# A softcap attention and maxout kernel: a fourth U buffer, and the reciprocal's transfers and multiplications moved in the written order

## The chip, the cores and the metric

The kernel runs on one core of a Trainium2 chip. The metric is the device time of one launch in microseconds (us), from start to end on that core. The time before is the median of three runs, and the profile is of one more execution of the same kernel.

In the profile the engines are called PE (the matrix engine), DVE (the vector engine), ACT (the scalar engine), POOL (GpSimd) and SP (the engine that issues nearly all transfers here). "SPq" is SP's instruction queue: its entries are the issues of transfers, not the transfers themselves.

## The reference

Two stages follow each other. The first is attention with a soft cap on the scores, for 8 batches of 12 heads with 448 rows of 64; the second is a layer on its 3584 rows of 768 that takes the larger of two products and multiplies it once more.

```python
scores = (1 / sqrt(64)) * (q @ k.T)
scores = cap * tanh(scores / cap)                  # cap = 30
attn = exp(scores - max(scores)); attn = attn / (sum(attn) + 1e-9)
x = (attn @ v)                                     # heads side by side: 3584 x 768
out = maximum(x @ w1, x @ w2) @ w_out              # 768 -> 1024 -> 768
```

## The kernel before

**Tiling.** Two heads make a pair (128 partitions), so there are N = 48 pairs, numbered i. Three pairs make a group g (16 groups), which is the unit of loading, casting and transposing. Two pairs make an iteration t of the main loop (line 523, NQ = 24 iterations); pair i = 2t is its first half, pair 2t + 1 its second. A "slot" in the text is such a half, numbered as the pairs are.

**Attention.** For each iteration PE makes the scores of the next one (`scores`, line 277), ACT takes tanh and then exp of them, both into bf16, and PE multiplies the exponentials with v (`pv`, line 325). Nothing is divided yet: `pv` copies the product to a float32 tile `U[t]` (line 351, on DVE) and the sums of the exponentials, which PE forms in `ss`, to a tile `st` (line 354). There are three buffers for U.

**The reciprocal's way.** The sums stand in rows of a 128 x 448 tile. A small transfer (the *gather*, line 357) packs them into 32 x 56, DVE takes the reciprocal (`invert`, line 363), a second transfer writes the result to memory (`rec_d`, line 365), and two more read it back, repeated over 64 partitions each (`spread`, line 371, `rec_b`). At last POOL multiplies U by rec_b into xT, the bf16 input of the second stage (`normalize`, line 383). So one iteration's reciprocal takes three stages of transfers, all issued from SP's queue, and each of them waits there for the one before.

**Loads and transposes.** From group 4 on, q and k of a group are loaded in float32 (`load`, lines 137 to 148), cast by POOL to bf16 in a tile kqf (`cast`), and turned by one crossbar transfer per group (`cross`, line 268) into qkT, which `scores` reads. v is loaded and cast. The groups before 4 are turned by PE (`transposes`).

**The second stage** (`moe`, line 388) is a generator for one batch: each step is one matmul. The main loop draws such steps between its own work with F(n), and the weights are made ready in the same way in iterations 1 to 4 (`turn_w2`, `premultiply`, and `subtract` on DVE). When the main loop is over, the rest of the steps run alone.

**What sets the order.** The kernel has a manual schedule: each engine, and SP's queue too, runs its instructions in the order in which the program writes them, and waits in front of each until what it needs is there. A list `todo` (lines 455 to 476) says in which slot a load, cast or transpose is written; `extra(i)` writes what is listed for slot i. With e = 3g for even g and 3g - 1 for odd g, k is loaded in slot e - 8 and q there or, for odd g, one slot on; they are cast in e - 6; the transpose and v's load stand in e - 4, v's cast in e - 2. In the steady state this gives a round of three iterations:

- iterations 5, 8, 11, 14, 17: a transpose, a v, a k and a q in one slot (called *heavy* below);
- iterations 6, 9, 12, 15, 18: a k and, half an iteration on, a q (*light*);
- iterations 7, 10, 13, 16, 19: a transpose and a v (*middle*).

Around these, an iteration t over 4 writes, in this order: spread(t - 2), extra(2t), pv(t, 0), normalize(t - 2), invert(t - 1), extra(2t + 1), and pv(t, 1) with the gather of t.

Of the kernel before, what the change touches and what calls it, by code (L numbers as in the profile page):

```python
# [10 lines left out]
def kernel(  # L11
# [11 lines left out]
    nc = tc.nc  # L23
    f32 = mybir.dt.float32
# [4 lines left out]
    B, H, S, D = q.shape  # L29
# [3 lines left out]
    P = 128  # L33
# [4 lines left out]
    NQ = N // 2  # L38
    Q0 = 4 * P
    NJ = 3  # L40
    NT = 4
# [7 lines left out]
    upool = ctx.enter_context(tc.tile_pool(name="upool", bufs=2))  # L49
# [227 lines left out]
    def scores(t, p, m0=0, m1=2):  # L277

        if m0 == 0:
            tanh[t, p] = att.tile([P, 4, S], bf16, name="tanh")  # L280
        if p == 2:
            s = s_psum.tile([P, 2, 512], f32, name="s")
        for m, (ab, j) in list(enumerate(PARTS[p]))[m0:m1]:
            i = 2 * t + ab
            g = i // L
            k0 = qkT[g][:, i % L, :, :].rearrange("p j c -> p (j c)")
            o = Q0 + (64 * (i // NP % 2) if g >= NT else 0)
            qTn = k0[:, o : o + S]
            if p == 2:
                nc.tensor.matmul(s[:, m, :S], k0[:, 3 * P : 4 * P], qTn)  # L290
                continue
            s = s_psum.tile([P, 2, 512], f32, name="s")
            for h in range(2):
                r = slice(64 * h, 64 * h + 64)
                nc.tensor.matmul(s[:, h, :S], k0[r, j * P : (j + 1) * P], qTn[r, :])  # L295
            nc.scalar.activation(tanh[t, p][:, 2 * m : 2 * m + 2, :], s[:, :, :S], AF.Tanh, scale=scale / cap)  # L296
        if p == 2:
            nc.scalar.activation(tanh[t, p][:, 0:2, :], s[:, :, :S], AF.Tanh, scale=scale / cap)  # L298

    def ex(t, p):  # L300
        n = 2 if p == 2 else 4
        expo[t, p] = att.tile([P, n, S], bf16, name=f"expo{p}", bufs=1 if p == 3 else 2)
        nc.scalar.activation(expo[t, p], tanh[t, p][:, 0:n, :], AF.Exp, scale=float(cap))  # L303

    def e_of(t, ab, j):
        p, m = LP[ab, j]
        return expo[t, p][:, m : m + (1 if j == NJ else 2), :]
# [3 lines left out]
    def add(t, ab, step):  # L311

        if t < NS or t >= NQ:
            return
        if t not in esum:
            esum[t] = att.tile([P, 4, S], bf16, name="esum")
        d = esum[t][:, 2 * ab : 2 * ab + 2, :]
        if step == 0:
            nc.vector.tensor_add(d, e_of(t, ab, 1 if ab else 0), e_of(t, ab, 2 if ab else 1))  # L319
        else:  # L320
            nc.vector.tensor_add(d, d, e_of(t, ab, 0 if ab else 2))  # L321

    U, sums, rec, recd = {}, {}, {}, {}

    def pv(t, ab):


        i = 2 * t + ab
        g, n = divmod(i, L)
        ps = pv_psum.tile([P, 512], f32, name="pv")  # L330
        for j in range(NJ):
            for h in range(2):
                r = slice(64 * h, 64 * h + 64)
                nc.tensor.matmul(  # L334
                    ps[r, :S], vp[g % 2][:, 2 * n + h, j, :], e_of(t, ab, j)[:, h, :], start=(j == 0), stop=False
                )
        if ab:
            ss = pv_psum.tile([P, 512], f32, name="ss")
            for m in range(2):
                nc.tensor.matmul(  # L340
                    ss[64 * m : 64 * m + 64, :S], ones2, expo[t, 2][:, m, :], start=True, stop=False
                )
            nj = NJ if t < NS else 1
            for j in range(nj):
                for m in range(4):
                    x = e_of(t, m // 2, j)[:, m % 2, :] if t < NS else esum[t][:, m, :]
                    nc.tensor.matmul(ss[32 * m : 32 * m + 32, :S], ones, x, start=False, stop=(j == nj - 1))  # L347
        nc.tensor.matmul(ps[:, :S], vl[g % 2][:, n, :], expo[t, 2][:, ab, :], start=False, stop=True)  # L348
        if ab == 0:
            U[t] = upool.tile([P, 2, S], f32, name="u", bufs=3)  # L350
        nc.vector.tensor_copy(U[t][:, ab, :], ps[:, :S])  # L351
        if ab:
            st = upool.tile([P, S], f32, name="st", bufs=1)
            nc.vector.tensor_copy(st, ss[:, :S])

            sums[t] = xpool.tile([32, 56], f32, name="sums")
            nc.sync.dma_start(
                out=sums[t], in_=st.rearrange("(m p) (a c) -> m p a c", p=32, a=8)[:, 0, :, :]
            )
# [7 lines left out]
    def spread(t):  # L367
        rec[t] = xpool.tile([P, 2, S], f32, name="rec_b")
        lines = recd[t].rearrange("(n h a) c -> h n (a c)", h=2, a=8)
        for h in range(2):  # L370
            nc.sync.dma_start(
                out=rec[t][64 * h : 64 * h + 64, :, :], in_=lines[h : h + 1, :, :].to_broadcast([64, 2, S])
            )
# [3 lines left out]
    def normalize(t, ab, eng=nc.gpsimd):  # L377
        i = 2 * t + ab
        b, hp = divmod(i, NP)
        if i % (2 * NP) == 0:  # L380
            xT[b // 2] = xpool.tile([P, NP, 2 * S], bf16, name="xT")
        cs = slice((b % 2) * S, (b % 2 + 1) * S)
        eng.tensor_mul(xT[b // 2][:, hp, cs], U[t][:, ab, :], rec[t][:, ab, :])  # L383
# [55 lines left out]
    def F(n):  # L439
        while n > 0 and fill_q:  # L440
            try:
                next(fill_q[0])
                n -= 1
            except StopIteration:
                fill_q.pop(0)
# [6 lines left out]
    def at(i, f, *a):  # L452
        todo[i].append((f, a))

    for g in range(2, NL):
        if g < NT:
            e = 0 if g == 2 else 1
            at(3 * g - 6 + e, load, g, "k")
            at(3 * g - 6 + e, load, g, "q")
            at(3 * g - 4 + e, load, g, "v")  # L460
            at(3 * g - 4, cast, nc.gpsimd, g, "k")
            at(3 * g - 4, cast, nc.gpsimd, g, "q")
            at(3 * g - 2, cast, nc.gpsimd, g, "v")
        else:
            e = 3 * g - g % 2
            at(e - 8, load, g, "k")
            at(e - 8 + g % 2, load, g, "q")
            at(e - 6, cast, nc.gpsimd, g, "k")
            at(e - 6, cast, nc.gpsimd, g, "q")
            at(e - 4, cross, g)  # L470
            at(e - 4, load, g, "v")
            at(e - 2, cast, nc.gpsimd, g, "v")
    at(1, load, 1, "v")
# [39 lines left out]
    def weights(i):  # L513
        if MS <= i < MS + KC:
            fill_q.append(turn_w2(i - MS))
        if MS < i <= MS + KC:
            fill_q.append(premultiply(i - MS - 1))

    def extra(i):
        for f, a in todo[i]:  # L520
            f(*a)

    for t in range(NQ):
        i = 2 * t
        more = t + 1 < NQ
        more8 = 1 if t >= 8 and more else 0
        weights(i)
        if t % 3 == 2 and t > 2:
            fill_q.append(moe(t // 3 - 1))
        if more:  # L530
            scores(t + 1, 0)
        ex(t, 3)
        F(2)
        add(t, 0, 1)
        F(2)
        if i + 3 < NT * L:
            transposes(i + 3)
        F(5 + more8 if more else 0)
        if t > 4:
            spread(t - 2)  # L540
        extra(i)
        F(6 if more else 3)
        if more:
            scores(t + 1, 1)
            ex(t + 1, 0)
        pv(t, 0)
        F(8 + more8)
        F(3 if more else 0)
        if MS < i <= MS + KC:
            subtract(i - MS - 1)  # L550
        if t > 4:
            normalize(t - 2, 0)
            normalize(t - 2, 1)
        if more:
            scores(t + 1, 2)
            ex(t + 1, 1)
        weights(i + 1)
        if i + 4 < NT * L:
            transposes(i + 4)
        F(2 + more8 if more else 0)  # L560
        add(t, 1, 0)
        F(4 if more else 2)
        add(t, 1, 1)
        F(2 if more else 0)
        if t > 4:
            invert(t - 1)
        elif t > 1:
            spread(t - 2)
        extra(i + 1)
        F(3 + more8 if more else 0)  # L570
        if more:
            scores(t + 1, 3)
            ex(t + 1, 2)
        pv(t, 1)
        F(4)
        if more:
            add(t + 1, 0, 0)
        F(3 if more else 0)
        if 0 < t < 5:
            invert(t - 1)  # L580
        if 1 < t < 5:
            normalize(t - 2, 0)
            normalize(t - 2, 1)
        if MS < i + 1 <= MS + KC:
            subtract(i - MS)
    F(6)
    spread(NQ - 2)
    F(10)
    invert(NQ - 1)
    F(16)  # L590
    spread(NQ - 1)
# [40 lines left out]
```

## Time and profile before

| what | value |
|---|---|
| median of three runs | 379.54 us (375.2 to 382.09) |
| span of the profiled execution | 379.2 us |
| mean granted PE clock | 0.980 of full speed |
| DVE busy | 200.6 us (53%) |
| ACT busy | 281.8 us (74%) |
| POOL busy | 150.1 us (40%) |
| transfers issued by SP | 71.1% of 16 engines' time, 67.99 MB |
| a u copy on DVE (line 351) | 624 ns, 48 of them |
| a multiplication on POOL (line 383) | 1238 ns, 48 of them |

How to read it: ACT's work ends with the last exponential at about 319 us; after that PE runs the remaining steps of the second stage alone. Up to there each iteration needs about 12 to 13 us. The share of a busy engine is an average over the start (loads and PE transposes), the middle (attention with matmul steps between) and the end (matmul steps alone), and these have different limits. The number of matmuls is fixed by the program, so an idle PE in the middle is time that isn't won back at the end.

### The profile page before, as it was taken

Reading aid. Unit: us, or ns where it says so; the run is one execution under the profiler, and the core shown is the slowest. Engines: PE = TensorE matmul, PEld = TensorE weight load, DVE = VectorE, ACT = ScalarE, POOL = GpSimd, SP = SyncE. Lnnn points to the kernel's source line nnn. Section 1 sums busy time; section 2 is a strip of 40 time slices with the busy share of each in tenths; the row PEclk is TensorE's granted clock in tenths of the full one; section 3 lists DMA queues with packets and bytes.
Section 4 is the critical chain, followed back from the end, with each engine's and each line's share of the span. In section 5 each row is a group of like instructions: output and inputs, shape, how many; then the busy total and the mean of one; then the engine's idle time right before and its main releaser. Section 6 shows DMA issues by size and latency. Waiting matters only on the chain.

```text
span 379.2 us, 6549 instructions
## 1 busy us (share of the span) xinstructions
PE 349.0 (92%) x2492; PEld 168.2 (44%) x2492; DVE 200.6 (53%) x348; ACT 281.8 (74%) x265; POOL 150.1 (40%) x188
## 2 busy tenths in 40 slices
PE   3677986898999999999999999999989999999996
PEld 2223443443444444444444454434434444555563
DVE  4223473567665676455745654557448556633421
ACT  4999986697999989998898899889958897000000
POOL 3734135637554445444562456243644302420000
PEclk9997898999999999999999999999989999999999
DMA  7999999996788987999698959896988132422022
GB/s 251 263 209 220 274 284 223 227 193 139 215 212 221 213 232 203 223 234 255 177 213 208 251 163 250 232 242 165 216 217 213 51 91 105 122 80 95 2 83 84
DMA packets 104464, 71.56 MB, mean 189 GB/s; under 512 B 58224, under 2 KB 99440, under 8 KB 104432
## 3 DMA queue, kind: packets, MB, share of 16 engines
q1 hardware_dynamic: 102480, 67.99, 71.1%
q0 software_dynamic: 1952, 3.15, 4.5%
q8 instruction: 19, 0.31, 0.4%
q14 instruction: 13, 0.11, 0.1%
HBM read 53.48 MB, written 11.18 MB: 171 GB/s over the span
## 4 chain that ended last, share of the span: by engine, by line
PE 65%; DMA 19%; DVE 5%; SPq 4%; ACT 3%; issue 2%; POOL 1%; POOLq 0%; DVEq 0%; ACTq 0%
PE mm L396 17%; PE mm L411 16%; PE mm L408 12%; PE pv L334 6%; DMA qkT<-kqf 6%; PE s L295 6%; DMA qr<-in_q_dram 6%; DMA vr<-in_v_dram 4%; DMA rec_b<-rec_d 3%; PE pv L348 3%; PE ss L347 2%; PE s L290 1%; DVE u L351 1%; ACT expo L303 1%; ACT tanh L296 1%
## 5 line engine op out<-in xcount | busy, mean ns | idle before, releaser
L296 ACT ACTIVATE tanh<-s 128x896 bf16<-128x896 f32 x144 | 124.3, 915 | 32.5 <-PE s L295 31.1
L303 ACT ACTIVATE expo<-tanh 128x1792 bf16<-128x1792 bf16 (+1 forms) x96 | 144.9, 1510 | 0.1
L383 POOL TENSOR_TENSOR xT<-u,rec_b 128x448 bf16<-128x448 f32 x48 | 58.4, 1238 | 101.1 <-DMA rec_b<-rec_d 81.2
L411 PE MATMUL mm<-wo_sb,gT 128*128 128x384 bf16 x448 | 86.8, 330 | 0.0
L396 PE MATMUL mm<-xT,wd_sb 128*128 128x448 bf16 x384 | 79.1, 354 | 2.7 <-POOL xT L383 1.3
L351 DVE COPY u<-pv 128x448 f32<-128x448 f32 x48 | 29.9, 624 | 91.0 <-PE pv L348 78.3
L408 PE MATMUL mm<-wm_sb,xT 128*128 128x384 bf16 x336 | 66.6, 326 | 0.2 <-DVE gT L400 0.2
L411 PEld LDWEIGHTS <-gT 128*128 128x128 bf16 x448 | 43.6, 99 | 31.1 <-issue 3.6
L415 DVE COPY osb<-mm 128x384 f32<-128x384 f32 x56 | 31.1, 555 | 46.3 <-PE mm L411 46.0
L396 PEld LDWEIGHTS <-wd_sb 128*128 128x128 bf16 x384 | 37.2, 98 | 38.4 <-issue 5.9
L295 PE MATMUL s<-qkT 64*128 64x448 bf16 x288 | 43.2, 371 | 11.1 <-ACT tanh L298 3.4
L400 DVE TENSOR_SCALAR gT<-mm 128x448 bf16<-128x448 f32 x64 | 39.1, 616 | 16.8 <-PE mm L396 16.6
L408 PEld LDWEIGHTS <-xT 128*128 128x128 bf16 x336 | 32.5, 98 | 23.3 <-issue 1.9
L334 PE MATMUL pv<-expo,vp 128*64 128x448 bf16 x288 | 37.5, 370 | 0.0
L158 POOL CAST vp<-vr 128x1152 bf16<-128x1152 f32 x15 | 18.0, 1201 | 46.8 <-DMA vr<-in_v_dram 43.5
L321 DVE TENSOR_TENSOR esum<-esum,expo 128x896 bf16<-128x896 bf16 x38 | 29.9, 787 | 1.5
L319 DVE TENSOR_TENSOR esum<-expo 128x896 bf16<-128x896 bf16 x38 | 26.6, 699 | 0.0
L295 PEld LDWEIGHTS <-qkT 64*128 64x128 bf16 x288 | 9.4, 95 | 36.8 <-issue 28.7
L298 ACT ACTIVATE tanh<-s 128x896 bf16<-128x896 f32 x24 | 22.0, 917 | 4.4 <-PE s L290 3.9
L334 PEld LDWEIGHTS <-vp 128*64 128x64 bf16 x288 | 12.4, 110 | 21.3 <-issue 15.2
L232 PE MATMUL mm<-wo_sb,w2T 128*128 128x384 bf16 x96 | 19.1, 334 | 1.4 <-DVE qkT L264 1.4
L178 POOL CAST kqf<-qr 128x1152 bf16<-128x1152 f32 x12 | 14.5, 1207 | 9.6 <-DMA qr<-in_q_dram 9.4
(56 smaller groups left out, 227.7 us busy)
## 6 DMA issues: line engine op xcount, KB each, us to landing
rec_b<-rec_d SPq DMA_DIRECT2D x48, 224.0 KB
kr<-in_k_dram SPq DMA_DIRECT2D x12, 576.0 KB
qr<-in_q_dram SPq DMA_DIRECT2D x12, 576.0 KB
vr<-in_v_dram SPq DMA_DIRECT2D x12, 576.0 KB
out_dram<-osb SPq DMA_DIRECT2D x17, 384.0 KB
out_dram<-osb SPq DMA_DIRECT2D x22, 192.0 KB
osb<-in_moe_w_dram SPq DMA_DIRECT2D x6, 512.0 KB
vr<-in_v_dram SPq DMA_DIRECT2D x8, 288.0 KB
```

Of the source, the lines that this page charges most:

```text
L295: nc.tensor.matmul(s[:, h, :S], k0[r, j * P : (j + 1) * P], qTn[r, :])
L296: nc.scalar.activation(tanh[t, p][:, 2 * m : 2 * m + 2, :], s[:, :, :S], AF.Tanh, scale=scale / cap)
L303: nc.scalar.activation(expo[t, p], tanh[t, p][:, 0:n, :], AF.Exp, scale=float(cap))
L321: nc.vector.tensor_add(d, d, e_of(t, ab, 0 if ab else 2))
L334: nc.tensor.matmul(ps[r, :S], vp[g % 2][:, 2 * n + h, j, :], e_of(t, ab, j)[:, h, :], start=(j == 0), stop=False)
L351: nc.vector.tensor_copy(U[t][:, ab, :], ps[:, :S])
L383: eng.tensor_mul(xT[b // 2][:, hp, cs], U[t][:, ab, :], rec[t][:, ab, :])
L396: nc.tensor.matmul(ps[:, :S], wd_sb[:, c, f * P : (f + 1) * P], x[:, c, cs], start=(c == 0), stop=(c == KC - 1))
L400: nc.vector.tensor_relu(g[:, f, cs], ps[:, :S])
L408: nc.tensor.matmul(ps[:, : DM // 2], x[:, c, ts], wm_sb[:, c, hs], start=(c == 0), stop=False)
L411: nc.tensor.matmul(ps[:, : DM // 2], g[:, f, ts], wo_sb[:, f, hs], start=False, stop=(f == FC - 1))
L415: nc.vector.tensor_copy(osb[:, hs], ps[:, : DM // 2])
```

## The change

Five edits to buffers and to the written order; no operation on data is added or taken away.

1. `upool` gets a fourth buffer for U, so that iteration t's first copy waits for the multiplication of t - 4 and not of t - 3.
2. Group 4's k and q are loaded in slot 5 and cast in slot 7, where before they were in 4 and 6. For odd groups from 5 on, q is loaded in the same slot as k and not one slot on.
3. `cross` is written first in the loop over groups. For groups that share a slot the order is by group, before and after.
4. spread(t - 1) is written right ahead of the second pv of iteration t, and so ahead of that iteration's gather; before, it was written in iteration t + 1, behind the gather.
5. normalize(t - 2) is written ahead of extra(2t), so that POOL multiplies before it casts; before it came behind. Iterations 2 to 4 and the end are fitted to this.

It is meant to bring the reciprocals sooner, so that POOL doesn't stand still with casts queued behind a multiplication, and to free DVE from waiting for a U buffer.

```diff
         if ab == 0:
-            U[t] = upool.tile([P, 2, S], f32, name="u", bufs=3)
+            U[t] = upool.tile([P, 2, S], f32, name="u", bufs=4)
...
             e = 3 * g - g % 2
-            at(e - 8, load, g, "k")
-            at(e - 8 + g % 2, load, g, "q")
-            at(e - 6, cast, nc.gpsimd, g, "k")
-            at(e - 6, cast, nc.gpsimd, g, "q")
+            first = g == NT
             at(e - 4, cross, g)
+            at(e - 8 + first, load, g, "k")
+            at(e - 8 + first, load, g, "q")
+            at(e - 6 + first, cast, nc.gpsimd, g, "k")
+            at(e - 6 + first, cast, nc.gpsimd, g, "q")
             at(e - 4, load, g, "v")
             at(e - 2, cast, nc.gpsimd, g, "v")
...
+        if t == 4:
+            spread(t - 2)
         if t > 4:
-            spread(t - 2)
+            normalize(t - 2, 0)
+            normalize(t - 2, 1)
         extra(i)
...
-        if t > 4:
+        if t == 4:
             normalize(t - 2, 0)
             normalize(t - 2, 1)
...
         if t > 4:
             invert(t - 1)
-        elif t > 1:
+        elif 1 < t < 4:
             spread(t - 2)
         extra(i + 1)
         F(3 + more8 if more else 0)
         if more:
             scores(t + 1, 3)
             ex(t + 1, 2)
+        if t > 4:
+            spread(t - 1)
         pv(t, 1)
...
         if 0 < t < 5:
             invert(t - 1)
-        if 1 < t < 5:
+        if t == 4:
+            spread(3)
+        if 1 < t < 4:
             normalize(t - 2, 0)
             normalize(t - 2, 1)
...
-    F(6)
-    spread(NQ - 2)
-    F(10)
+    F(16)
     invert(NQ - 1)
```

## The prediction

> **What bounds the kernel now.** I read the page's busy times and slices first, then PE's timeline for its idle stretches, then what ended them on DVE, and last SP's own queue and its waits.
>
> ```profile
> PE 349.0 (92%) x2492; PEld 168.2 (44%) x2492; DVE 200.6 (53%) x348; ACT 281.8 (74%) x265; POOL 150.1 (40%) x188
> PE   3677986898999999999999999999989999999996
> PEclk9997898999999999999999999999989999999999
> DMA  7999999996788987999698959896988132422022
> ```
>
> PE is busy 349.0 of 379.2 us. From about 90 us on it hardly stops: in windows of 20 us it is busy 20.00 four times between 100 and 200, and all its idle time between 100 and 320 us adds up to 3.5 us. The 48 matmuls of line 396 that start at 325.45 take 9.08 us, 189 ns each, so this busy PE is at its full rate. What can be won lies in the few idle pieces, and in the clock dips beside them.
>
> ```profile
> 64.47 0.90 PE L262 MATMUL mm<-ident,kqf 64*64 64x64 bf16 x26 [3.66 <-DVE wm_sb L237]
> 88.21 0.35 PE L396 MATMUL mm<-xT,wd_sb 128*128 128x448 bf16 x1 [1.26 <-POOL xT L383]
> 277.61 0.55 PE L295 MATMUL s<-qkT 64*128 64x448 bf16 x4 [1.85 <-DMA qkT<-kqf]
> 63.33 0.62 DVE L351 COPY u<-pv 128x448 f32<-128x448 f32 x1 [5.60 <-POOL xT L383]
> 260.73 0.49 DVE L363 RECIPROCAL rec_s<-sums 32x56 f32<-32x56 f32 x1 [0.40 <-DMA sums<-st]
> ```
>
> The bracket is the idle time in front, and what ended it. The fourth line explains the first: DVE stood 5.60 us at iteration 3's first u copy, because three U buffers made it wait for POOL's first multiplication, and PE's next PSUM tile was behind that on DVE. The last line matters most: in iteration 18 the reciprocal is already reached by DVE before its gather has landed.
>
> ```profile
> 241.62 1.27 SPq L371 DMA_DIRECT2D rec_b<-rec_d  x2
> 242.99 4.64 SPq L268 DMA_TRANSPOSE qkT<-kqf  x1
> 247.68 0.57 SPq L137 DMA_DIRECT2D vr<-in_v_dram  x1
> 248.30 1.29 SPq L148 DMA_DIRECT2D vr<-in_v_dram  x2
> 249.63 0.60 SPq L137 DMA_DIRECT2D kr<-in_k_dram  x1
> 250.28 1.26 SPq L148 DMA_DIRECT2D kr<-in_k_dram  x2
> 251.59 0.60 SPq L137 DMA_DIRECT2D qr<-in_q_dram  x1
> 252.23 0.99 SPq L142 DMA_DIRECT2D qr<-in_q_dram  x1
> 253.32 1.13 SPq L431 DMA_DIRECT2D out_dram<-osb  x1
> 254.55 0.73 SPq L365 DMA_DIRECT2D rec_d<-rec_s  x1
> 255.37 0.61 SPq L357 DMA_DIRECT2D sums<-st  x1
> 260.50 1.26 SPq L371 DMA_DIRECT2D rec_b<-rec_d  x2
> ...
> SPq L371 <- DMA rec_d<-rec_s: 31.4, 14, 4.4
> POOL xT L383 <- DMA rec_b<-rec_d: 81.2, 20, 9.5
> ```
>
> This is SP in a heavy iteration. It issues without a pause from 241.62 to 255.98, then stands 4.5 us until rec_d has landed (31.4 us over the run). The spreads of the heavy iterations start at 103.34, 143.01, 181.79, 221.19 and 260.50: a round of three iterations takes 39.3 us. In the round 202.79 to 241.62 (38.8 us) SP's pauses are only 3.7 (for rec_d), 0.6 (for st) and 1.9 (for rec_d), so 32.7 us is issuing. SP is the second resource without slack: at 230.61 and 269.47 the transposes go out so late that PE waits 0.45 us at 237.5 and 1.85 us at 277.6. POOL's 81.2 us of waiting cost PE little, for POOL has 60% of the span free.
>
> **What the Trainium skill says.** "DMA: Bandwidth & Descriptors", in "Anatomy of one DMA", gives about 2.0 us as a transfer's fixed cost (for the GpSimd path) and says that a wait is taken by the issuing sequencer before dispatch, not by the DMA engines; so everything behind it in the queue waits too. The trace agrees: nothing is issued in the 4.5 us before 260.50. The same page, "Queues, rings and completion order", says that each engine takes descriptors in ring order, so a 7 KB write stands behind the loads issued before it. Here rec_d of 254.55 was free to be read back only at 260.50, and the DMA engines were 90% busy up to about 257.5. "TensorE: Matmul & The Clock Gate", "What's actually happening", says that the clock is halved after an idle window of about 3.4 us. After the 3.66 us pause the 26 small transposes took 0.90 us, against 0.60 at 54.89; after the 1.85 us pause eight matmuls of line 411 took 2.56 us, against 1.30 elsewhere, though that pause is shorter than the page's window.
>
> **The change part by part.**
>
> The fourth U buffer and group 4's later load: iteration 3's copy no longer waits. DVE gets 5.60 us, PE 3.66 us of idle and about 1.3 us of slow clock (0.3 on the transposes, 0.75 on the four matmuls of line 232 behind them, the rest on line 221). Spread(0) goes out ahead of 1.3 MB of group 4, so it lands before the 60.1 us of now. The 1.26 us at 88.21 goes too, as normalize(2) is written half an iteration sooner. Sum: 5 to 7 us sooner by iteration 5, if SP follows. The 0.6 us that later first multiplications could cost POOL lie beside its free 60%.
>
> cross first in the loop over groups: the slot lists are unchanged by it, since each slot is still ordered by group. Nothing. The q load of odd groups moves ahead of rec_d in the light iterations; the same issue time, 1.25 us.
>
> normalize ahead of the casts: POOL's two multiplications take 2.2 us and wait for nothing now, as their spread was issued half an iteration before. Casts start up to 4 us sooner, but they are done about 10 us ahead of their transpose already (group 14's at 260.7, its transpose at 269.47). Nothing on the path.
>
> spread ahead of the gather: the added wait. SP now issues rec_d(t - 1) and then stands until it has landed, with the gather of t, the next iteration's transpose and its loads queued behind. Before, a q load (1.3), the gather (0.6) and sometimes an output (0.5 to 1.5) lay in that time. Latency from the end of rec_d's issue to the spread: heavy 3.9, 4.4, 3.75, 4.45, 5.2, mean 4.3; middle 2.15, 3.0, 3.2, 2.9, mean 2.8; light at most 2.7, 4.4, 4.2, 3.8. For the light one I take 3.0, between the 2.0 of the skill's page and the 4.4. Sum 10.1 us a round against 6.2 now. Issue time: 32.7, or 30.8 if each entry took its shortest seen time; I take 31.7, since longer rounds leave the rings emptier. Round: 31.7 + 10.1 = 41.8 us. Both ends, with the shortest and the longest latencies (3.75 + 2.0 + 2.15 and 5.2 + 4.4 + 3.2): 30.8 + 7.9 = 38.7 and 32.7 + 12.8 = 45.5.
>
> Who waits: the gather goes out behind the spread, so iteration t + 1's reciprocal waits, and DVE stands in front of it with PSUM copies behind it, so PE stops a moment later. Direct check, with all else as now: the gathers of the heavy iterations would go out at 104.6, 144.3, 183.5, 222.5 and 261.8 and land 2 to 3.5 us later; DVE now takes these reciprocals at 107.1, 145.0, 183.3, 220.4 and 260.7. Stalls of 0 to 1.1, 1.3 to 2.8, 2.2 to 3.7, 4.1 to 5.6 and 3.1 to 4.6: 11 to 18 us in all.
>
> The sum: in iteration 5 the new order starts its transpose at about 85 (88.7 now: attention 5 us sooner, less SP's new wait for rec_d(3)), issues 10.2 us, rec_d 0.5, waits 4.3, spread 1.3, gather 0.7: at 102. Four rounds of 41.8 later, in iteration 17, that is 269.2; the gather lands at about 271.7, the reciprocal now comes at 260.7. Attention is 11 us late there. After it only two transposes and one k and q are left, each still bound by the same chain, and the end is PE's fixed work. 379.5 + 11.4 = about 391 us.
>
> **Rivals.**
>
> A: rec_d lands quickly, because the rings are emptier, and a round stays what it is (39.3). Then the 5 us won are mostly kept for PE, less the gather's later place (1 to 3 us): 375 to 379, and up to 382 at a round of 39.7. For it: 1.4 us from rec_d at 85.92 to the spread at 87.35, with little queued. Against it: no heavy latency under 3.75.
>
> B, faster: SP isn't the limit, PE's rate sets the round (three iterations of 12.7, 38.1 us). Then 5 to 7 us at the start and 1.85 + 1.3 us at 277 fall away: 369 to 372. For it: PE is 100% busy in most windows. Against it: SP's pauses are 6 us a round and all but 0.6 are that latency, which grows.
>
> C: the light latency is 4.4 and issuing stays at 32.7: a round of 44.2; 102 + 4 x 44.2 + 2.5 = 281 against 260.7: as much as 20 us late, 399.
>
> **How the numbers follow.** The forecast has 0.5 (384 to 395), C 0.1, A 0.26, B 0.14. Range 374 to 401: it holds the forecast, C and most of A, and leaves out B and the worst of C. Slower by over 2% is over 387.1: C and most of the forecast, 0.59. Faster is under 371.9, B: 0.14. Within 2%: A and the forecast's low end, 0.27.
>
> **What would show it.** Right: no u wait on POOL near 60 us and no 3.66 us PE pause; POOL's wait for rec_b far below 81.2; SP's wait for rec_d well over 31.4 us and nearer 55 to 65; reciprocals on DVE that wait for the gather, in iterations 6, 9, 12, 15, 18, some 2 to 4 us each; heavy spreads about 42 us apart. Wrong: heavy spreads 38 to 39 us apart and no wait of the reciprocal, which means that SP had room or rec_d lands in about 2 us.

## The result, and the profile after

The changed kernel takes 404.9 us (median; 402.0 to 405.65) against 378.8 us before in the same runs: a ratio of 1.071 (95% interval 1.061 to 1.081). It is slower, as forecast, but by 26 us and not by 12, and it lies above the range.

The same parts of the page as before, now of the changed kernel, then its waits of the engines, and those of SP's queue (total us, times, longest):

```profile
PE 356.6 (88%) x2492; PEld 169.7 (42%) x2492; DVE 209.1 (52%) x348; ACT 281.6 (70%) x265; POOL 156.7 (39%) x188
PE   4678898879998997699987999799959999899996
PEclk9996999969999999889999999899999999999999
```

```profile
POOL xT L383 <- DMA rec_b<-rec_d: 137.6, 19, 16.2
DVE rec_s L363 <- DMA sums<-st: 32.4, 11, 6.4
```

```profile
SPq L371 <- DMA rec_d<-rec_s: 73.8, 23, 5.8
```

The profiled span grew by 24.0 us, from 379.2 to 403.2. On PE it divides like this: the same 2492 matmuls are busy 7.6 us longer (the third line shows the granted clock, with digits under 9 beside the pauses), and PE's idle time went from 30.2 to 46.6 us. SP's wait for rec_d is 73.8 us where it was 31.4, and the reciprocals, which waited 0.4 us in all, now wait 32.4. POOL's wait for rec_b, which the change was to shorten, rose from 81.2 to 137.6.

Where PE now stands, from its timeline (start, duration, instruction, and in brackets the pause in front):

```profile
83.06 0.93 PE L295 MATMUL s<-qkT 64*128 64x448 bf16 x4 [3.81 <-DMA qkT<-kqf]
...
168.16 0.93 PE L295 MATMUL s<-qkT 64*128 64x448 bf16 x4 [3.72 <-DMA qkT<-kqf]
213.67 0.55 PE L295 MATMUL s<-qkT 64*128 64x448 bf16 x4 [3.87 <-DMA qkT<-kqf]
...
300.44 0.92 PE L295 MATMUL s<-qkT 64*128 64x448 bf16 x4 [4.63 <-DMA qkT<-kqf]
```

It waits for a group's transpose once in each round (the two left out are 1.54 us at 123.38 and 2.69 us at 255.02), 20.3 us in all. Before, two such waits of 0.45 and 1.85 us were all. The 3.66 us pause behind the u copy is gone, and the first line shows what came in its place: 3.81 us at the transpose of group 4.

SP's queue from the small write of heavy iteration 17 to the spread of the light iteration behind it:

```profile
273.17 0.37 SPq L365 DMA_DIRECT2D rec_d<-rec_s  x1
279.42 1.25 SPq L371 DMA_DIRECT2D rec_b<-rec_d  x2
280.76 0.59 SPq L357 DMA_DIRECT2D sums<-st  x1
281.40 0.44 SPq L137 DMA_DIRECT2D kr<-in_k_dram  x1
...
283.88 0.60 SPq L142 DMA_DIRECT2D qr<-in_q_dram  x1
284.58 0.84 SPq L365 DMA_DIRECT2D rec_d<-rec_s  x1
290.25 2.20 SPq L371 DMA_DIRECT2D rec_b<-rec_d  x2
```

DVE's timeline has the answer to the gather that went out at 280.76:

```profile
283.96 0.49 DVE L363 RECIPROCAL rec_s<-sums 32x56 f32<-32x56 f32 x1 [5.28 <-DMA sums<-st]
```

Behind rec_d nothing is issued for 5.9 us, and then in the light iteration for another 4.8. The light iteration's write goes out directly behind a k and a q. DVE stood 5.28 us at a reciprocal that it took at 260.73 before.

A measure that serves for all the kernels below: the *round* is the mean distance of the spreads that wait for the writes of iterations 5, 8, 11, 14 and 17, and SP's *pauses* are the idle times of its queue (over 0.15 us) in those four rounds, divided by four and sorted by what was issued after them. Each ratio is against runs of the kernel before in the same session. Medians are over all runs of a kernel and ratios over those in its fast state, which matters most in one row: of "changed, casts first" two of four runs were slow, and the two fast ones took 398.2 and 401.6 us.

| kernel | median us | ratio (95%) | round | pause ahead of spreads | ahead of transposes |
|---|---|---|---|---|---|
| before | 378.8 | 1 | 39.3 | 5.3 | 0 |
| changed | 404.9 | 1.071 (1.061 to 1.081) | 43.9 | 11.6 | 0.5 |
| before, spread ahead of gather | 388.8 | 1.027 (1.019 to 1.036) | 41.8 | 7.7 | 0 |
| before, multiplications ahead of casts | 391.0 | 1.035 (1.025 to 1.045) | 41.1 | 5.0 | 4.3 |
| before, q early | 386.7 | 1.022 (1.012 to 1.033) | 41.0 | 8.0 | 0 |
| before, fourth U buffer | 379.1 | 1.000 (0.997 to 1.003) | 39.0 | 5.2 | 0 |
| before, fourth U buffer, group 4 later | 379.9 | 1.002 (0.999 to 1.005) | 39.6 | 5.5 | 0 |
| changed, gather first | 400.9 | 1.060 (1.053 to 1.067) | 43.6 | 9.3 | 0.8 |
| changed, casts first | 403.3 | 1.057 (1.041 to 1.074) | 43.5 | 11.4 | 0 |
| changed, q late | 397.0 | 1.047 (1.039 to 1.056) | 43.1 | 8.2 | 3.4 |
| changed, transpose of group 4 first | 398.9 | 1.055 (1.046 to 1.065) | 43.6 | 11.7 | 0.3 |
| changed, q late, transpose of group 4 first | 395.1 | 1.045 (1.038 to 1.053) | 42.6 | 8.5 | 2.9 |
| changed, q late, casts first | 389.2 | 1.032 (1.025 to 1.039) | 41.1 | 8.3 | 0 |
| changed, rec_d from POOL | 413.1 | 1.090 (1.080 to 1.100) | not used | not used | not used |
| before, fourth U, rec_d from POOL | 377.1 | 0.997 (0.994 to 0.999) | 37.8 | 1.9 | 0 |
| before, fourth U, spread behind a transpose or k | 379.8 | 1.005 (1.002 to 1.007) | 39.5 | 1.6 | 0 |

### The profile page after: what moved, and what is told of

The parts are those of the page before. It is cut to its first block, busy times and chain, and to the rows that moved or that the text cites. A ratio compares the mean times of both kernels' runs of the same rounds, so it can differ in the third digit from the quotient of the medians.

```text
span 403.2 us, 6537 instructions
## 1 busy us (share of the span) xinstructions
PE 356.6 (88%) x2492; PEld 169.7 (42%) x2492; DVE 209.1 (52%) x348; ACT 281.6 (70%) x265; POOL 156.7 (39%) x188
## 4 chain that ended last, share of the span: by engine, by line
PE 50%; DMA 25%; DVE 7%; SPq 6%; ACT 5%; POOL 4%; issue 3%; POOLq 0%; DVEq 0%
PE mm L396 14%; PE mm L411 11%; DMA rec_d<-rec_s 8%; PE mm L408 8%; DMA qkT<-kqf 8%; PE s L295 5%; DMA rec_b<-rec_d 5%; PE pv L334 4%; ACT expo L303 2%; ACT tanh L296 2%; PE pv L348 2%; DMA sums<-st 2%; PE mm L232 2%; POOL xT L383 2%; SPq L148 1%
## 5 line engine op out<-in xcount | busy, mean ns | idle before, releaser
L383 POOL TENSOR_TENSOR xT<-u,rec_b 128x448 bf16<-128x448 f32 x48 | 58.6, 1240 | 160.9 <-DMA rec_b<-rec_d 137.6
L411 PE MATMUL mm<-wo_sb,gT 128*128 128x384 bf16 x448 | 88.8, 335 | 0.0
L396 PE MATMUL mm<-xT,wd_sb 128*128 128x448 bf16 x384 | 80.3, 357 | 1.5 <-DVE gT L400 1.2
L408 PE MATMUL mm<-wm_sb,xT 128*128 128x384 bf16 x336 | 69.0, 335 | 4.0 <-DVE osb L415 3.8
L295 PE MATMUL s<-qkT 64*128 64x448 bf16 x288 | 44.8, 381 | 29.0 <-DMA qkT<-kqf 20.3
L411 PEld LDWEIGHTS <-gT 128*128 128x128 bf16 x448 | 44.3, 100 | 32.8 <-issue 6.0
L321 DVE TENSOR_TENSOR esum<-esum,expo 128x896 bf16<-128x896 bf16 x38 | 33.3, 875 | 1.5
L319 DVE TENSOR_TENSOR esum<-expo 128x896 bf16<-128x896 bf16 x38 | 30.8, 810 | 0.0
L363 DVE RECIPROCAL rec_s<-sums 32x56 f32<-32x56 f32 x24 | 11.7, 486 | 32.4 <-DMA sums<-st 32.4
L158 POOL CAST vp<-vr 128x1152 bf16<-128x1152 f32 x15 | 20.7, 1380 | 16.8 <-DMA vr<-in_v_dram 8.6
```

The source lines that it names most:

```text
L396: nc.tensor.matmul(ps[:, :S], wd_sb[:, c, f * P : (f + 1) * P], x[:, c, cs], start=(c == 0), stop=(c == KC - 1))
L408: nc.tensor.matmul(ps[:, : DM // 2], x[:, c, ts], wm_sb[:, c, hs], start=(c == 0), stop=False)
L411: nc.tensor.matmul(ps[:, : DM // 2], g[:, f, ts], wo_sb[:, f, hs], start=False, stop=(f == FC - 1))
```

## The experiments

**Which edit costs the time.** Theory 1 is the prediction's: the landing of rec_d is paid in SP's queue, with the gather and the next transpose behind it. The first run undoes its edit, the fourth part of the change; three others do one part alone or undo the q load. Theories and rivals have the numbers that the recorded expectations give them; a rival's number doesn't mean the same in every run.

```diff
             ex(t + 1, 2)
-        if t > 4:
-            spread(t - 1)
         pv(t, 1)
+        if t > 4:
+            spread(t - 1)
```

> The changed kernel with one edit: from iteration 5 on, spread(t - 1) is written right behind the second pv of iteration t, so that the gather goes out ahead of it; all other engines keep the changed order. Theory 1 (SP's round: the landing of rec_d is paid three times a round with gather, transpose and loads queued behind): the heavy spreads come back to 39 to 40.5 us apart, the reciprocal's wait for the gather falls from 32.4 to under 6 us, and the time to 379 to 386 us; some of the loss before iteration 5 stays (PE's 3.8 us at 83 us). Rival 2 (POOL's new order, multiplications ahead of casts, costs the time): nothing of POOL is changed here, so 400 us or more stays.

It took 400.9 us. The reciprocals' wait fell as expected, from 32.4 to 3.3 us, but the round did not come back (43.6). So DVE's wait at the reciprocal, for all its 32 us, was not what held the kernel: SP's pauses were still 9.3 us a round, and PE waited for the transposes instead. Theory 1 is wrong in blaming the place of the gather alone.

The same edit on the kernel before:

```diff
-        if t > 4:
+        if t == 5:
             spread(t - 2)
         extra(i)
...
+        if t > 4:
+            spread(t - 1)
         pv(t, 1)
...
-    F(6)
-    spread(NQ - 2)
-    F(10)
+    F(16)
     invert(NQ - 1)
```

> The kernel before with the spread of iterations 5 and later moved ahead of the gather, and nothing else (three U buffers, old load slots, q of odd groups half an iteration later, old place of the multiplications). Theory 1: most of the loss comes from this edit: heavy spreads 42 to 43.5 us apart, reciprocals waiting for the gather, 393 to 401 us; a little under the changed kernel, as the q load still fills part of the light iteration's landing. Rival 2 (POOL's order or the start make the loss): 378 to 384 us.

388.8 us: 9 us slower, with a round of 41.8 us. The edit costs time by itself, though less than the 393 us that theory 1 gave as the least.

```diff
-            U[t] = upool.tile([P, 2, S], f32, name="u", bufs=3)
+            U[t] = upool.tile([P, 2, S], f32, name="u", bufs=4)
```

> The kernel before with a fourth U buffer alone. Theory 1: the 5.6 us wait of iteration 3's u copy and PE's 3.66 us pause go, with some 1.3 us of slow clock; 373 to 376 us if SP's queue follows. Rival 3 (the start is set by SP's queue and the loads, so the wait only moves): PE stops as long a little later, for the transpose of group 4 or 5, and the time stays at 378 to 380 us.

379.1 us, a ratio of 1.000. The wait went; the time did not. PE's pause moved to the first matmuls on xT, from 1.26 us at 88.21 to this (its timeline):

```profile
85.06 0.35 PE L396 MATMUL mm<-xT,wd_sb 128*128 128x448 bf16 x1 [2.44 <-POOL xT L383]
86.15 0.92 PE L396 MATMUL mm<-xT,wd_sb 128*128 128x448 bf16 x4 [0.74 <-POOL xT L383]
```

PE came to them some 4 us sooner (at 82.6 and not at 87.0), but POOL's multiplications of iteration 2 ended only 2.1 us sooner (at 86.1 and not at 88.2). That accounts for a part of the 5 us; rival 3 is right in that the wait moves, though it moved to xT and not to a transpose. The profiled run of this kernel took 376.4 us, less than its median, so its span isn't compared with that of the kernel before; below only its order and its rounds are used.

```diff
-            at(e - 8 + first, load, g, "q")
+            at(e - 8 + (first or g % 2), load, g, "q")
```

> The changed kernel with q of the odd groups over 4 loaded half an iteration after k again, so that it is issued between rec_d and the spread of the light iteration. Theory 1, with the light iteration's landing as the mis-sized term (4.4 to 5.1 us measured, 3.0 forecast): q's 1.25 us of issue lies inside the landing and 0.77 MB less stands ahead of rec_d, so the light landing costs 2 to 3 us less of SP's time; rounds of 41 to 42.5 us instead of 43.9 and 394 to 399 us. Rival 4 (the landing is a fixed time and does not depend on what is queued): the round falls by 1.25 us at most, 398 to 401 us; and if q's place does nothing, 404 us.

397.0 us, 8 us less than the changed kernel. The pause ahead of spreads fell by 3.4 us a round: in the light iterations the spread now follows the end of rec_d's issue after 2.2 to 2.8 us, where it was 4.4 to 5.1. (The q load is 0.69 MB by the profile's sizes, 576 and 96 KB, and not 0.77.) But the round fell only from 43.9 to 43.1, for another pause appeared that had been nearly absent: 3.4 us ahead of the transposes. From SP's queue, a light iteration of this kernel:

```profile
237.31 1.47 SPq L371 DMA_DIRECT2D rec_b<-rec_d  x2
238.88 0.59 SPq L357 DMA_DIRECT2D sums<-st  x1
242.69 3.57 SPq L268 DMA_TRANSPOSE qkT<-kqf  x1
```

SP is ready at 239.5 and the transpose waits 3.2 us more: the group's last cast ends at 242.67, behind multiplications that POOL could start only at 234.04, after 13.06 us of waiting for rec_b.

**POOL's order and the early q, each alone.** On the kernel before:

```diff
         if t > 4:
             spread(t - 2)
+            normalize(t - 2, 0)
+            normalize(t - 2, 1)
         extra(i)
...
-        if t > 4:
-            normalize(t - 2, 0)
-            normalize(t - 2, 1)
```

> The kernel before with one edit: from iteration 5 on the two multiplications of t - 2 are written right behind their spread and ahead of the casts of slot 2t, instead of behind them. Moving the gather back behind nothing (the run with the gather first) left 401 us of the changed kernel's 405, with POOL standing up to 16 us for rec_b. Theory 5, formed from that: POOL stands for the late reciprocal with casts behind it, so the casts of k and q end after the time at which SP could issue the transpose, and v's casts come late too: group 14's casts end near 273 us instead of 260.7, against its transpose at 269.5. Some 3 us a round, 388 to 396 us, SP pausing ahead of middle transposes. Theory 1 alone (only the landings of rec_d in SP's queue count): 377 to 382 us.

391.0 us: the edit that the prediction put at nothing costs 12 us by itself, more than any other. First POOL's timeline, then SP's queue of the same run:

```profile
231.78 2.23 POOL L383 TENSOR_TENSOR xT<-u,rec_b 128x448 bf16<-128x448 f32 x2 [12.56 <-DMA rec_b<-rec_d]
233.95 1.55 POOL L158 CAST vp<-vr 128x1152 bf16<-128x1152 f32 x1
...
236.65 1.15 POOL L178 CAST kqf<-kr 128x1152 bf16<-128x1152 f32 x1
...
239.65 0.90 POOL L183 CAST kqf<-qr 64x384 bf16<-64x384 f32 x1
```

```profile
234.27 1.31 SPq L371 DMA_DIRECT2D rec_b<-rec_d  x2
240.57 3.57 SPq L268 DMA_TRANSPOSE qkT<-kqf  x1
```

POOL stood 12.56 us for rec_b, then ran 2.2 us of multiplications, 2.7 us of v's casts and 3.9 us of k's and q's, up to 240.55. SP had been free since 235.6, and the transpose went out at 240.57, as the last cast ended. Theory 5 holds.

In the changed kernel the same order was then undone:

```diff
-        if t > 4:
-            normalize(t - 2, 0)
-            normalize(t - 2, 1)
         extra(i)
...
-        if t == 4:
+        if t > 3:
             normalize(t - 2, 0)
```

> The changed kernel with the multiplications of iterations 5 and later back in their old place, behind the casts and the first pv; the spread stays ahead of the gather and q of the odd groups stays early. Theory 5: POOL's casts are no longer behind rec_b, SP's pauses ahead of the middle transposes (about 1 us each) go, 395 to 400 us; what is left comes from the spread ahead of the gather and the early q. Theory 1 alone: POOL's order does nothing, 403 to 406 us.

The median is 403.3 us, but the ratio is 1.057 against 1.071, with intervals that overlap. So the time settles nothing between theory 5 and theory 1 alone. The profile shows that little came of it in the middle of the kernel: POOL's wait for rec_b fell to 74.9 us and the pause ahead of the transposes went, but the pause for rec_d stayed (11.4 us a round of 11.6), and the round fell by 0.4 us only.

```diff
-            at(e - 8 + g % 2, load, g, "q")
+            at(e - 8 + 0, load, g, "q")
```

> The kernel before with one edit: q of the odd groups over 4 is loaded in the same slot as k. Theory 6 (the light landing): q's issue of 1.25 us leaves the shadow of rec_d's landing and 0.77 MB more stands ahead of rec_d, so SP's pause ahead of the light spread grows from about 0.6 to 3 us; rounds of 41 to 42 us, 386 to 392 us. Rival 4 (q's place does nothing, SP has room in the light iteration): 378 to 381 us.

386.7 us, 8 us slower, pause ahead of spreads 8.0: theory 6 as expected. The landing ahead of the light spreads was 4.1 to 5.4 us here.

The parts of the change that were meant for the start:

```diff
-            U[t] = upool.tile([P, 2, S], f32, name="u", bufs=3)
+            U[t] = upool.tile([P, 2, S], f32, name="u", bufs=4)
...
-            at(e - 8, load, g, "k")
-            at(e - 8 + g % 2, load, g, "q")
+            first = g == NT
+            at(e - 8 + first, load, g, "k")
+            at(e - 8 + (first or g % 2), load, g, "q")
...
-            at(e - 6, cast, nc.gpsimd, g, "k")
-            at(e - 6, cast, nc.gpsimd, g, "q")
+            at(e - 6 + first, cast, nc.gpsimd, g, "k")
+            at(e - 6 + first, cast, nc.gpsimd, g, "q")
```

> The kernel before with the fourth U buffer and group 4's k and q one slot later, everything else as before. Theory 1: the start's gain of some 4 to 5 us shows by iteration 5 (second pv of iteration 5 ends near 93 us instead of 97.8), and the rounds keep it as they are no slower than before; 373 to 377 us. Rival 3 (the later group 4 makes its transpose late, and PE waits for it near 80 us, as in the changed kernel): 379 to 384 us.

379.9 us: neither the gain of theory 1 nor a loss that could be told from none. In its profile PE stops 1.9 us at 77.6 for a wm_sb copy and 1.8 us at 85.9 for xT. The start has a row of waits close behind each other, and taking the first out lets the next ones show.

**What the landing depends on.** In the next two runs the 7 KB write is issued from POOL's queue, first in the changed kernel:

```diff
         recd[t] = dram.tile([32, 56], f32, name="rec_d")
-        nc.sync.dma_start(out=recd[t], in_=r)
+        nc.gpsimd.dma_start(out=recd[t], in_=r)
```

> The changed kernel with the small write rec_d issued from POOL's queue and not from SP's; the two spreads that wait for it stay on SP. The runs so far show SP's pause ahead of the spreads at 5.3 us a round in the kernel before, 7.7 with the spread ahead of the gather alone, 8.0 with the early q alone and 11.6 in the changed kernel. Theory 1 (the write stands behind the loads that SP queued ahead of it): from another queue it passes them and lands in about 2 us, SP's pause falls below 7 us a round, rounds 38 to 40.5 us, 380 to 390 us. Rival 4 (the landing is long because all 16 transfer engines are busy with loads, whatever queue the write comes from): pause of 10 us or more, rounds of 43 us, 399 to 405 us.

413.1 us, the slowest of all, and neither side's number. (The profiled run lies above the other runs of this kernel by 4 to 8 us, so only the order within it is used.) In the light iteration after iteration 11 POOL has this order, and SP's queue has nothing between a q and the spread:

```profile
199.15 2.23 POOL L383 TENSOR_TENSOR xT<-u,rec_b 128x448 bf16<-128x448 f32 x2 [11.92 <-DMA rec_b<-rec_d]
...
207.56 0.54 POOL L365 DMA_DIRECT2D rec_d<-rec_s  x1
```

```profile
197.74 0.81 SPq L142 DMA_DIRECT2D qr<-in_q_dram  x1
209.26 1.23 SPq L371 DMA_DIRECT2D rec_b<-rec_d  x2
```

From the end of the write's issue, at 208.10, to the spread it is 1.2 us, where it was over 4 from SP's queue. That doesn't show that the write passes the loads, for none were left to pass: SP had issued nothing since 198.55, and from 205.0 to 207.5 the transfers moved 7 GB/s. The write stands behind POOL's multiplications and casts, which wait for the spread before, so now one more link of the reciprocal's way waits for the last one. The test of the landing was spoiled by POOL's order; the next run, with the old order, is the clean one.

The second is the kernel before with this edit and the fourth U buffer:

> The kernel before with the fourth U buffer and rec_d issued from POOL's queue. Theory 1: SP's pause of 5.3 us a round falls to 2 us or less, rounds fall to PE's own 38 us and the waits for qkT near 237 and 277 us go, 370 to 376 us. Rival 4: as before, 378 to 381 us. A rival on POOL's side: the write stands there behind casts that wait for loads, the reciprocal gets later, 380 us or more.

377.1 us. The pause ahead of spreads fell from 5.2 (fourth U buffer alone) to 1.9 us, the round from 39.0 to 37.8, and PE's waits for qkT are all but gone (0.3 us in all). Theory 1's pause came, but its reason did not: the write lands hardly faster than before. Here is one heavy iteration, first in SP's queue with the fourth U buffer alone:

```profile
135.36 0.61 SPq L365 DMA_DIRECT2D rec_d<-rec_s  x1
...
140.62 1.26 SPq L371 DMA_DIRECT2D rec_b<-rec_d  x2
```

Then in this run, from POOL's timeline and from SP's queue:

```profile
132.99 0.54 POOL L365 DMA_DIRECT2D rec_d<-rec_s  x1 [1.72 <-DVE rec_s L363]
```

```profile
138.07 1.26 SPq L371 DMA_DIRECT2D rec_b<-rec_d  x2
```

And this run's 24 writes from the start of their issue, from the view of the tile rec_d:

```profile
DMA to landing us min/median/max: 1.6/3.7/5.9
```

DVE's reciprocal ended at 131.41 in the first and at 132.69 in the second. In SP's queue the write had to wait 3.95 us for its turn, behind v, k and q; from POOL's queue it went out after 0.3 us. From the end of its issue to the spread it then took 4.65 and 4.54 us. In the five heavy iterations the wait for the turn fell from 5.1 to 0.35 us on average, while the landing, from the end of the issue, was 4.1 to 5.7 us (mean 4.8, to the spread) from SP's queue and 3.4 to 4.5 (mean 4.1) from POOL's. So most of what this run saved is the write's turn in SP's full queue, and not its landing. For the landing itself rival 4 fits better: it is long while loads are being moved, from either queue. At 297.11, with almost nothing moving, the write from POOL's queue landed after 1.6 us; at 232.55, with 356, 363, 129 and 6 GB/s in the four microseconds behind it, after 3.7.

The time gained is small: 0.3% on the kernel before, and the interval overlaps that of the fourth U buffer alone. PE is busy for 150.8 of the four rounds' 151.4 us here, and in the kernel before it already was for 156.1 of 157.2, so there was next to nothing to win. SP now waits 3.8 us a round ahead of the gathers, for sums that aren't made yet.

The landing can also be hidden by other issues, in the kernel before with the fourth U buffer:

```diff
+        lead = [x for x in todo[i] if t > 4 and x[0] in (cross, load)][:1]
+        for f, a in lead:
+            f(*a)
         if t > 4:
             spread(t - 2)
-        extra(i)
+        for x in todo[i]:
+            if x not in lead:
+                x[0](*x[1])
```

> The kernel before with the fourth U buffer and, from iteration 5 on, spread(t - 2) written behind the transpose of that slot (or behind the load of k in the light iterations) and not ahead of it. Theory 1: the transpose's 4.6 us of issue lie inside the landing of rec_d, SP's pause falls from 5.3 to about 1 us a round, transposes go out 3 to 4 us sooner, and PE's waits for qkT near 237 and 277 us go; 371 to 377 us. Rival: rec_b comes 5 us later, POOL stands longer with casts behind it and PE waits for xT at a batch's first matmul; 380 to 386 us.

379.8 us, ratio 1.005 (1.002 to 1.007). SP's wait for rec_d fell from 34.5 us over the run to 9.0, as expected, and yet nothing came of it; POOL's wait for rec_b rose from 69.8 to 122.7 us. PE's waits for qkT, 2.1 us with the fourth U buffer alone, went too, and its waits for xT rose from 3.2 to 4.0 us. A shorter pause by a later reciprocal was no gain here.

**The start, and two terms together.**

```diff
-        if t == 4:
-            spread(t - 2)
         if t > 4:
             normalize(t - 2, 0)
             normalize(t - 2, 1)
         extra(i)
+        if t == 4:
+            spread(t - 2)
```

> The changed kernel with iteration 4's spread(2) written behind the transpose and load of group 4 and not ahead of them. This is the start's share: in the changed kernel the transpose of group 4 goes out at 77.2 us behind a pause of 5.8 us for rec_d(2), PE waits 3.8 us for it at 83 us and runs slow behind that. Theory 7 (the start is a loss of its own): the transpose goes out near 70 us, the pause at 83 us goes, the first heavy spread comes 3 to 5 us sooner, rounds stay at 43.9 us, 399 to 402 us. Rival (SP's queue takes it all back by iteration 5): 403 to 406 us.

398.9 us, 6 us less. The transpose of group 4 went out at 73.1 and not at 77.2, PE's pause at 83 us went, and the first heavy spread came 1.8 us sooner (theory 7 said 3 to 5), with nearly the same round (43.6).

This edit and the late q together, both as shown above:

> The changed kernel with two terms taken out that the forecast had too small or not at all: q of the odd groups half an iteration later again (alone: 397.0 us of 404.9), and iteration 4's spread(2) behind the transpose of group 4 (alone: 398.9). If these two are the whole of what the forecast of 391 us missed, and add up, this one takes 389 to 393 us. If they overlap in SP's queue, 394 to 397 us.

395.1 us: 9.8 us less than the changed kernel, where the two edits alone gave 7.9 and 6.0. That points to an overlap, though the intervals of the ratios are too wide to show one. Together the two don't reach the forecast's 391.

And the late q with the casts first, both as shown above:

> The changed kernel with q of the odd groups late again and the multiplications back behind the casts. In the changed kernel SP pauses 11.6 us a round for rec_d and 0.5 for the casts ahead of its transposes; with q late it is 8.2 and 3.4. Theory 8 (the wait for the casts is real, but hidden behind the longer one; of two waits in one round only the longer counts): here the 3.4 us go, rounds of 39.5 to 41.5 us, 385 to 391 us, although the same edit without the late q brought only 1.6 us. Rival: POOL's order costs nothing beside the early spread, 395 to 398 us.

389.2 us, in the middle of theory 8's numbers. The pause ahead of the transposes is gone and the pause ahead of spreads unchanged (8.3), so POOL's order is worth 2.0 us a round here (43.1 to 41.1), against 0.4 without the late q (43.9 to 43.5). The ratios don't show this difference: the same edit takes 1.047 to 1.032 here and 1.071 to 1.057 there. By SP's pauses the wait for the casts was in the changed kernel all along, behind a longer one: 8.2 + 3.4 with q late is the 11.6 that stood there for rec_d alone. The times neither confirm nor contradict it.

## Why the prediction was right and wrong

**Right.** The direction and its cause: SP's queue has no slack in the changed kernel, and the landings of rec_d set the round. Its term for issuing, 31.7 us a round, is what was measured (43.9 less pauses of 11.6, 0.5 and 0.1); the reason that it gave for the size was not tested. The landings of heavy iterations were 3.7 to 5.9, mean 4.5 (4.3 forecast), those of middle ones 2.8 (2.8). That the spread ahead of the gather alone gave a round of 41.8 us, the number forecast for the whole change, is chance: its pause ahead of spreads is 7.7 us, and the forecast had 10.1.

**Not shown: ring order.** The prediction took from the Trainium skill's "DMA: Bandwidth & Descriptors", "Queues, rings and completion order", that the write stands behind the loads of its own queue. The same section says that a transfer engine goes round between the rows of different queues packet by packet, which lets one expect that from POOL's queue a small write passes the loads. Measured there, it took 3.9 to 5.0 us from the start of its issue in the heavy iterations, so the order of its own queue explains at most a small part of the landing (from the end of the issue 4.8 us on average from SP's queue, 4.1 from POOL's).

**Wrong: the light landing.** It was taken as 3.0, between 2.0 and 4.4; it measured 4.4 to 5.1, mean 4.6. The four values that it was taken from leave out the first light iteration, where it was at most 5.1. And they were measured with q behind rec_d; the change moves q's load ahead of it, which was called "the same issue time". So its bytes are still being moved when the write is issued: in the five microseconds from the light write at 284.58 on the transfers moved 326, 203, 334, 132 and 19 GB/s. With q behind rec_d again the light spread follows after 2.2 to 2.8 us. Early q alone cost 8 us on the kernel before, and taking it back gave 8 us. Rival C had this landing at 4.4 and a round of 44.2 us, close to the 43.9 measured, and was given a chance of 0.1.

**Wrong: the way to PE.** The prediction let PE lose its time behind DVE, which stands at a reciprocal whose gather is late. DVE did stand there, 32.4 us in all, but with the gather first this wait fell to 3.3 us and the round stayed at 43.6. What PE waits for is the transpose of a group, 20.3 us in six waits against 2.3 in two, because SP issues it late. The prediction named the transpose among what is queued behind the landing, but didn't follow it to PE.

**Wrong: multiplications ahead of casts at nothing.** The prediction said that they "wait for nothing now" and that the casts are about 10 us ahead of their transpose. The spread is only half an iteration sooner in the order written, and SP issues it late; so POOL waited up to 16.2 us. Alone the edit cost 12 us. In the changed kernel's pauses it showed little (0.5 us ahead of transposes), and with q late 3.4 us appeared there. So taking the early q back shortened the round by less than it shortened the pause, and the round came under the forecast's 41.8 us only where both were undone (41.1 us, 389.2 us).

**Wrong: the start.** Iteration 5's gather was forecast at 102 and came at 105.1. The spread(2) ahead of group 4's transpose, which the prediction did not price, paused SP for 5.8 us and made PE stand 3.81 us, and the gain from the U buffer was gone by then. In the kernel before, that gain wasn't there at all: a fourth U buffer alone gave a ratio of 1.000.

**The sum.** Iteration 17's gather was put at 269.2 and came at 280.8: 3.1 us are the start's and 4 x 2.1 = 8.4 the rounds'. Of a round's 2.1, 1.5 is in the pause ahead of spreads (11.6 against 10.1), 1.3 of it at the light landing and the rest at the heavy ones, and 0.6 ahead of transposes and gathers. (The 6.2 us that the prediction set against its 10.1 are one round's and hold 0.6 for st; over four rounds the kernel before has 5.3 ahead of spreads. Its 11.4 us are 11.0 by its own terms, and rival C's 399 us are 400.) DVE's reciprocal then came 23.2 us later than before, as the profiled span did (24.0). The signs of being wrong given beforehand did not show. Of the right ones POOL's wait for rec_b went the other way, and SP's wait for rec_d (73.8 us, 55 to 65 forecast) and the heavy spreads (43.9 us apart, 42 forecast) went beyond their numbers.

**Open.** The three edits of the steady state cost 9, 12 and 8 us alone and 26 us together with the rest; how much of the 26 belongs to which can't be said, as they share one round. The fourth U buffer's 5 us at the start were not followed to the end of the main loop. And why the write from POOL's queue doesn't pass the loads is not shown by any run here.

## What to carry to other kernels

Treat the queue of the engine that issues the transfers as an engine with a busy share: here issuing took 32.8 of a round's 39.3 us before the change, and a pause that grew by 2.4 us a round (the spread ahead of the gather alone) made the round 2.5 us longer. Between a small write and the transfer that reads it back, other issues hide the landing; moving a load from there to ahead of the write also made the landing longer. Hiding it pays only as long as what waits for the result can bear the delay. A small write that is waited for can be taken out of a full queue: what this saved here was the wait for its turn, and not its landing. And when an edit seems to cost nothing, ask what is longer than it at that place: undoing it alone may show little, while doing it alone on the old kernel shows its price.

## What the runs showed of the hardware

- From the end of the write's issue to the spread that waits for it, a 7 KB write from SP's queue took 2.0 to 3.5 us behind a transpose and a v, 3.6 to 6.1 behind a k and a q, and 1.1 with little queued.
- From POOL's queue, counted from the start of its issue, the same write landed after 1.6 to 5.9 us (median 3.7) in the kernel before with the fourth U buffer: 3.9 to 5.0 in the heavy iterations, and 1.6 with almost nothing moving.
- The PE clock fell after the longer pauses for transposes: behind the pause of 4.63 us at 300.44 the granted clock was 0.53 from 300.4 to 304.0, and six matmuls of line 408 took 2.10 us, against 1.14 elsewhere. In the kernel before it was 0.51 from 279 to 281 us, behind a pause of 1.85 us.
